# Matmuls without a use between the first attention units, and two expert weights asked for ahead of the attention's loop

## The chip, the cores and the metric

The kernel runs on one core of a Trainium2 chip. The metric is the device time of one execution in microseconds (us); the time before is the median of three runs. Beside it stands one execution taken by the hardware profiler, from which all rows below come. GB/s and MB are powers of ten, KB is 1024 bytes.

## What is computed

The reference has three stages. A linear attention with a decaying state runs over 4 batches, 8 heads, 768 positions and a head size of 48; its output, as 3072 tokens of 384 features, goes through a soft mixture of 8 experts with 4 slots each, and that through a feed-forward block with a squared ReLU.

```python
for t in range(S):                                   # attention, S = 768
    cur = np.einsum('bhd,bhe->bhde', u[None] * kt, vt)
    y[:, :, t] = np.einsum('bhd,bhde->bhe', rt, state + cur)
    state = w[None, :, :, None] * state + np.einsum('bhd,bhe->bhde', kt, vt)
...
logits = x @ phi                                     # experts: softmax over tokens in, over slots out
slot_input = softmax_over_tokens(logits).T @ x
slot_out[e] = np.maximum(slot_input[e] @ w1[e], 0.0) @ w2[e]     # 8 experts
x = softmax_over_slots(logits) @ slot_out
...
h = x @ w_in                                         # feed-forward, 384 -> 2048 -> 384
r = np.maximum(h, 0.0)
out = (r * r) @ w_out
```

## The kernel before

The order of the work is written out by hand: each engine, and SyncE's queue of transfers, runs its instructions in the order in which the program names them. The attention is cut into 16 units (one batch and two heads each; four units make a batch), each of 6 chunks of 128 positions. A unit's inputs come in four transfers: `load_t` brings the transposed keys and queries (two halves of 384 KB, line 92), `load_n` the natural keys, queries and values (448 and 416 KB, line 96, where the second half holds the rest of the queries and all values). There are four buffers for units (`NB = 4`), so unit n+4 is loaded into the buffer that unit n leaves; its loads are asked for at the end of iteration n, and each waits until TensorE has read what it overwrites. The first four units are asked for at the start, with the small `phi` between them. SyncE issues all of these transfers, and at most eight of them are under way: each waits also for the one eight places before it.

The work on unit n is: `bonus` (line 236 on, two GpSimd products; needs both halves of `load_n`), `decay` (line 232, VectorE, one for the keys, one for the queries), `weigh` (line 242, VectorE, needs the bonus), `keys` (line 248, GpSimd), `diag` (line 254, GpSimd, needs weigh), `A` (line 264, TensorE, two halves), `strict` (line 270, VectorE, copies A's result under a mask), `KV` (line 278, TensorE, needs keys), `scan` (line 283, VectorE), `Y` (lines 301 and 307, TensorE), and `X` and `L` (lines 320 and 335, TensorE: transposes and logits). An iteration n of the loop (line 440) runs A's second half and Y of unit n, keys, weigh, diag, KV, scan and A's first half of unit n+1, and bonus and the first decay of unit n+2. On GpSimd that is keys(n+1), two diags of n+1, bonus(n+2); on VectorE decay(n+1), strict(n) and so on stand behind weigh(n+1). "KV(5)" below is KV of unit 5; "strict(4,1)" is the second half of unit 4. In every fourth iteration a batch's softmax work (`soft_max` to `slots_norm`) is added.

The experts' weights are 16 transfers of 1536 KB each (`load_weight`, line 171 for w1 and 173 for w2). Nine of them have buffers of their own from the start (slots 4 to 12); they are asked for in the loop, each behind a unit's loads, in the iterations n = 0, 2, 3, 5, 6, 8, 9, 10, 11. The others follow as buffers come free: of the last units, and, behind the attention, of a pool ("post") that takes the place of the attention's tiles. There also stand the loads of w_in (line 137) and w_out (line 147). TensorE's last block, line 817, is the feed-forward's second product.

`keep_clock(n)` (line 220) is n matmuls of the identity with itself into a PSUM tile that nobody reads; each is two instructions on TensorE. It shares the tile of `X` (tag "tr", one buffer).

Of the kernel before, what the change touches and what calls it, by code (L numbers as in the profile page):

```python
# [29 lines left out]
def rwkv_softmoe_ffn(ctx: ExitStack, tc: tile.TileContext, tr, krv, wt, u, phi, w1, w2, w_in, w_out, out):  # L30
# [29 lines left out]
    def ps(tag):  # L60
        cnt[0] += 1
        return psum.tile([128, 512], F32, name=f"ps_{tag}{cnt[0]}", tag=tag, bufs=BANKS[tag])

    def wk(shape, tag, bufs, dt=F32, pool=None):
        cnt[0] += 1
        return (pool or work).tile(shape, dt, name=f"{tag}_{cnt[0]}", tag=tag, bufs=bufs)
# [3 lines left out]
    def take(i, dt=F32, cols=3072):  # L70
        cnt[0] += 1
        slots[i] = const.tile([128, SLOT[i]], dt, name=f"slot{i}_{cnt[0]}", tag=f"slot{i}", bufs=1)[:, :cols]
        return slots[i]
# [7 lines left out]
    def t_view(n):  # L81

        return units[n % NB][:112, :2 * S].rearrange("p (m c t) -> p m c t", m=2, c=NC)

    def n_view(n):

        return units[n % NB][:, 2 * S:].rearrange("p (m c h d) -> p m c h d", m=3, c=NC, h=2)
# [74 lines left out]
    def load_weight(i):  # L162
        kind, e = W[i]
        if str(home[i]).startswith("post"):
            cnt[0] += 1
            t = post.tile([128, 3072], F32, name=f"post_{cnt[0]}", tag=home[i], bufs=1)
        else:
            t = take(home[i])
        if kind == "w1":
            t = t.rearrange("p (c f) -> p c f", c=3)  # L170
            nc.sync.dma_start(t, w1[e].rearrange("(c p) f -> p c f", p=128))
        else:
            nc.sync.dma_start(t.rearrange("p (k f) -> p k f", k=3), w2[e].rearrange("k p f -> p k f"))
            t = t.rearrange("p (c d) -> p c d", c=8)
        wt_of[W[i]] = t
# [21 lines left out]
    for i in range(6):  # L197
        n = 1 << i
# [21 lines left out]
    def keep_clock(n):  # L220

        if n:
            p = ps("tr")
        for _ in range(n):
            nc.tensor.matmul(p[:, :256], ident, ident.unsqueeze(1).to_broadcast([128, 2, 128]), start=True, stop=True)


    def decay(n, m):

        x = t_view(n)[:, m]  # L230
        t = tab[:, n % NP] if m else tab[:, n % NP, ::-1]
        nc.vector.tensor_tensor(x, x, t.unsqueeze(1).to_broadcast([112, NC, 128]), ALU.mult)  # L232
# [7 lines left out]
    def weigh(n):  # L240
        dg = wk([128, NC, 2], "dg", 2)
        nc.vector.reduce_sum(dg, n_view(n)[:, 1], axis=AX.X)
        st[n, "dg"] = dg

    def keys(n, eng=nc.gpsimd):

        kv_ = n_view(n)[:, 0]
        eng.tensor_tensor(kv_, kv_, pkn[:, n % NP].unsqueeze(1).to_broadcast([128, NC, 2, D]), ALU.mult)

    def diag(n, g):  # L250
        at = wk([128, GC, 2, 128], "AT", 3, pool=att)
        st[n, "AT", g] = at
        dg = st[n, "dg"][:, GC * g:GC * (g + 1)]
        nc.gpsimd.affine_select(out=at.rearrange("p c h t -> p (c h) t"),  # L254
                                in_=dg.rearrange("p c h -> p (c h)").unsqueeze(2).to_broadcast([128, 2 * GC, 128]),
                                pattern=[[0, 2 * GC], [1, 128]], compare_op=ALU.is_equal, fill=0.0, base=0, channel_multiplier=-1)

    def A(n, g):
        tv = t_view(n)
        p = [ps("A")[:, :GC * 128].rearrange("p (c t) -> p c t", c=GC) for _ in range(2)]  # L260
        for i in range(GC):
            for h in range(2):
                rows = slice(64 * h, 64 * h + D)
                nc.tensor.matmul(p[h][:, i], tv[rows, 1, GC * g + i], tv[rows, 0, GC * g + i], start=True, stop=True)  # L264
        st[n, "A", g] = p

    def strict(n, g):
        at, p = st[n, "AT", g], st.pop((n, "A", g))
        for h in range(2):
            nc.vector.copy_predicated(at[:, :, h], mask.unsqueeze(1).to_broadcast([128, GC, 128]), p[h])  # L270
# [16 lines left out]
    def Y(n, g):  # L287
        vv, tv = n_view(n)[:, 2], t_view(n)
        at, s = st.pop((n, "AT", g)), SB[n % 2]

        p = [y.rearrange("p (c t) -> p c t", t=128) for y in yp]
        chunks = range(GC * g, GC * (g + 1))
        at_of = lambda c, j: p[c % 2][64 * j:64 * j + D, (c - chunks[c % 2 != chunks[0] % 2]) // 2]
        opened = set()
        for c in chunks:
            for h in range(2 if c > 0 else 0):
                rows, j = slice(64 * h, 64 * h + D), (h + c) % 2  # L300
                nc.tensor.matmul(at_of(c, j), s[rows, c], tv[rows, 0, c],  # L301
                                 start=(c % 2, j) not in opened, stop=True, skip_group_check=True)
                opened.add((c % 2, j))
        for c in chunks:
            for j in range(2):
                h = (j + c) % 2
                nc.tensor.matmul(at_of(c, j), vv[:, c, h], at[:, c - GC * g, h],  # L307
                                 start=False, stop=True, skip_group_check=True)
        if g == 0:
            st[n, "xT"] = wk([112, NC, 128], "xT", 2, pool=att)  # L310
        for k in range(2):
            c0 = chunks[k]
            nc.scalar.copy(st[n, "xT"][:, c0:GC * (g + 1):2], p[c0 % 2][:112, :len(chunks[k::2])])  # L313
# [34 lines left out]
    def soft_exp(b):  # L348

        eT = wk([96, 2, 256], "eT", 1)  # L350
        st["eT", b] = eT
        nc.scalar.activation(eT[:, 0], st["lg", b][:96, :256], AF.Exp, bias=st["nm", b])
        nc.scalar.copy(eT[:, 1], st["lg", b][:96, :256])
        if 0 < b < B - 1:
            new = st["new", b]
            fa, fb = wk([96, 1], "fa", 2), wk([96, 1], "fb", 2)
            nc.scalar.activation(fa, nmx[:, 0:1], AF.Exp, bias=new, scale=-1.0)
            nc.scalar.activation(fb, st["nm", b], AF.Exp, bias=new, scale=-1.0)
            nc.scalar.copy(nmx[:, 0:1], new)
            st["f", b] = fa, fb  # L360
# [56 lines left out]
    bonus(0)  # L417
    decay(0, 1)
    decay(0, 0)
    keep_clock(6)  # L420

    pp = ps("lg")
    for a in range(NP):
        nc.tensor.transpose(pp[:, a * 128:a * 128 + 112], tabs[:, a], ident[:112, :112])
    nc.scalar.copy(pkn, pp.rearrange("p (a b d) -> p a b d", a=NP, b=2)[:, :, :, :D])
    A(0, 0)
    weigh(0)
    diag(0, 0)
    keys(0, nc.vector)
# [6 lines left out]
        nc.gpsimd.memset(xn[i][:, :, DM:DM + 1], 1.0)  # L436
    bonus(1)
    decay(1, 0)
    nload = 0
    for n in range(NU):  # L440
        nxt = n + 1 < NU
        if n == 2:

            sel = const.tile([128, 4, NS], F32, name="sel")
            nc.vector.reduce_sum(sel, ident.rearrange("p (q s) -> p s q", q=4).unsqueeze(1).to_broadcast([128, 4, NS, 4]), axis=AX.X)
            rm = const.tile([128, E], F32, name="rm")
            nc.vector.reduce_sum(rm, ident.rearrange("p (q e j) -> p e q j", q=4, e=E), axis=AX.XY)
            ones = const.tile([1, 4], F32, name="ones")
            nc.gpsimd.memset(ones, 1.0)

        b, j = divmod(n, NP)
        b -= 1
        A(n, 1)
        if nxt:
            keys(n + 1)
            weigh(n + 1)
            diag(n + 1, 0)
            decay(n + 1, 1)
        strict(n, 1)
        if n > 0:  # L460
            X(n - 1, 0)
        if b >= 0 and j == 1:
            soft_exp(b)
        Y(n, 0)
        if b >= 0 and j == 2:
            soft_sum(b)
            slots_exp(b)
        if nxt:
            KV(n + 1)
            diag(n + 1, 1)  # L470
        if n > 0:
            L(n - 1)

        if nxt:
            A(n + 1, 0)
            scan(n + 1)
            strict(n + 1, 0)
        if n > 0:
            X(n - 1, 1)
        if not nxt:  # L480
            L(n, (0,))
            X(n, 0)
        Y(n, 1)
        if b >= 0 and j == 1:
            soft_turn(b)
        if n + 2 < NU:
            bonus(n + 2)
            decay(n + 2, 0)
        if b >= 0 and j == 0:
            soft_max(b)  # L490
        if b >= 0 and j == 2:
            slots_norm(b)
        if n + NB < NU:
            load_t(n + NB)
            load_n(n + NB)
            if n not in (1, 4, 7):
                load_weight(nload)
                nload += 1
        elif n == NU - 2:
            load_win(0)  # L500
        else:
            load_weight(nload)
            nload += 1
# [382 lines left out]
```

## Time and profile before

| | |
|---|---|
| time, median of 3 runs | 401.37 us (400.80 to 401.72) |
| the profiled execution, its own time | 400.18 us |
| its span, first to last instruction | 398.5 us |
| mean granted TensorE clock | 0.973 |
| TensorE busy | 381.7 us (96% of the span) |
| VectorE busy | 280.2 us (70%) |
| ScalarE busy | 211.7 us (53%) |
| GpSimd busy | 114.8 us (29%, nearly all in the first 120 us) |
| transfers | 70.81 MB, mean 178 GB/s over the span |

PE is TensorE's matmuls, PEld its weight loads, DVE VectorE, ACT ScalarE, POOL GpSimd, SP SyncE; SPq is SyncE's sequencer, which issues the transfers. L264 is line 264 of the kernel. Times inside the trace count from the span's start. Matmuls are pipelined and their ends are modelled, so a TensorE that is busy throughout is not one at its peak. The span runs to the last instruction; the execution's own time is 1.7 us longer.

### The profile page before, as it was taken

To read this page: it belongs to the slowest core of one execution; us is meant where nothing else is said; L and a number is where in the kernel's file an instruction comes from. 1 tells how busy PE (TensorE), PEld (TensorE's weight loads), DVE (VectorE), ACT (ScalarE), POOL (GpSimd) and SP (SyncE) were. 2 spreads that over 40 slices of the span, in tenths; PEclk is the share of its full clock that TensorE was granted. 3 is DMA by queue.
4 is the path that set the end of the run, shared out by engine and by line. 5 is a ranking of instruction groups with operands and counts; after the bars stand their busy time and mean duration, and the time that the engine had idled before them with its cause. 6 is when DMAs were issued, how large, how long until landed. Compare 5 with 4: busy or idle time off the path is not lost.

```text
span 398.5 us, 8194 instructions
## 1 busy us (share of the span) xinstructions
PE 381.7 (96%) x3219; PEld 294.2 (74%) x3219; DVE 280.2 (70%) x495; ACT 211.7 (53%) x465; POOL 114.8 (29%) x110
## 2 busy tenths in 40 slices
PE   5799999999999999789999999999999999999995
PEld 3677777767766564668787888888888888888884
DVE  5769897879974564799998567666566676566563
ACT  2224453453444451678888876555554564554552
POOL 3869997986870001122323120000000000000000
PEclk8559999999999999999999999999999999999999
DMA  7999999999995899913333202100000040000004
GB/s 245 344 320 343 389 407 403 404 404 406 405 383 188 307 410 405 375 47 102 85 100 87 63 0 104 56 0 2 0 0 2 0 159 2 0 0 2 0 0 158
DMA packets 25989, 70.81 MB, mean 178 GB/s; under 512 B 3680, under 2 KB 6112, under 8 KB 25952
## 3 DMA queue, kind: packets, MB, share of 16 engines
q1 hardware_dynamic: 25808, 70.10, 47.2%
q10 hardware_dynamic: 144, 0.20, 0.5%
q8 instruction: 25, 0.41, 0.4%
q14 instruction: 12, 0.10, 0.1%
HBM read 64.78 MB, written 4.72 MB: 174 GB/s over the span
## 4 chain that ended last, share of the span: by engine, by line
PE 80%; DMA 9%; DVE 6%; POOL 2%; issue 1%; ACT 1%; SPq 0%; POOLq 0%; ACTq 0%; DVEq 0%
PE ps_Y L817 16%; PE ps_A L817 16%; PE ps_kv L817 8%; PE ps_lg L817 8%; PE ps_A L264 7%; DMA wo<-in_w_out_dram 7%; PE ps_Y L307 5%; PE ps_Y L301 3%; PE ps_tr L320 3%; PE ps_tr L725 3%; PE ps_tab L725 3%; PE ps_lg L335 2%; DMA slot<-in_krv_dram 2%; PE ps_kv L278 2%; PE ps_tr L378 1%
## 5 line engine op out<-in xcount | busy, mean ns | idle before, releaser
L817 PE MATMUL ps_Y<-slot,slot 128*128 128x512 f32 x288 | 111.7, 395 | 0.0
L750 DVE TENSOR_TENSOR slot<-gg,slot 128x512 fp32r<-128x512 f32 (+1 forms) x97 | 66.5, 685 | 49.2 <-ACT slot L747 48.3
L817 PE MATMUL ps_A<-slot,slot 128*128 128x512 f32 x288 | 88.9, 393 | 0.6 <-DVE slot L682 0.6
L747 ACT CAST slot<-gg 128x512 fp32r<-128x512 f32 (+1 forms) x97 | 59.8, 618 | 50.5 <-DVE gg L744 49.9
L817 PEld LDWEIGHTS ps_A<-slot,slot 128*128 128x128 f32 x288 | 54.0, 188 | 13.2 <-DVE slot L682 1.0
L817 PEld LDWEIGHTS ps_Y<-slot,slot 128*128 128x128 f32 x288 | 54.1, 188 | 12.6 <-issue 0.6
L744 DVE TENSOR_TENSOR gg<-hr 128x512 f32<-128x512 f32 (+1 forms) x71 | 49.0, 691 | 14.3 <-ACT hr L737 14.2
L817 PE MATMUL ps_kv<-slot,slot 128*128 128x512 f32 x144 | 55.7, 394 | 0.0
L817 PE MATMUL ps_lg<-slot,slot 128*128 128x512 f32 x144 | 55.4, 391 | 0.0
L623 POOL TENSOR_TENSOR slot<-wf,slot 128x384 fp32r<-128x384 f32 x16 | 19.1, 1196 | 97.5 <-ACT slot L618 97.5
L270 DVE COPY_PREDICATED AT<-mask,ps_A 128x384 f32<-128x384 int32 x64 | 33.8, 583 | 9.2 <-PE ps_A L264 8.4
L264 PE MATMUL ps_A<-slot 48*128 48x128 f32 x384 | 36.2, 310 | 2.9 <-DVE slot L232 1.8
L264 PEld LDWEIGHTS ps_A<-slot 48*128 48x128 f32 x384 | 28.7, 204 | 10.3 <-DVE AT L270 3.6
L737 ACT ACTIVATE hr<-ps_tab 128x512 f32<-128x512 f32 x48 | 28.7, 599 | 12.9 <-PE ps_tab L725 12.9
L737 ACT ACTIVATE hr<-ps_tr 128x512 f32<-128x512 f32 (+1 forms) x49 | 28.8, 590 | 12.4 <-PE ps_tr L725 12.4
L313 ACT COPY xT<-ps_Y 112x256 f32<-112x256 f32 x64 | 17.4, 324 | 28.0 <-PE ps_Y L307 27.8
L254 POOL TENSOR_SCALAR_AFFINE_SELECT AT<-dg 128x768 f32<-128x768 f32 x32 | 28.0, 886 | 13.2 <-PE ps_Y L307 8.4
L817 PEld LDWEIGHTS ps_kv<-slot,slot 128*128 128x128 f32 x144 | 27.1, 188 | 6.2
L817 PEld LDWEIGHTS ps_lg<-slot,slot 128*128 128x128 f32 x144 | 27.0, 188 | 5.9
L232 DVE TENSOR_TENSOR slot<-slot,ps_tab 112x768 f32<-112x768 f32 x32 | 30.1, 941 | 0.6 <-DMA slot<-in_tr_dram 0.6
L307 PE MATMUL ps_Y<-AT,slot 128*48 128x128 f32 x384 | 29.6, 293 | 0.0
L307 PEld LDWEIGHTS ps_Y<-AT,slot 128*48 128x48 f32 x384 | 20.8, 129 | 6.5 <-issue 5.9
(168 smaller groups left out, 502.3 us busy)
## 6 DMA issues: line engine op xcount, KB each, us to landing
slot<-in_w_dram SPq DMA_DIRECT2D x14, 1536.0 KB, 11.1
slot<-in_tr_dram SPq DMA_DIRECT2D x32, 384.0 KB, 7.5
slot<-in_krv_dram SPq DMA_DIRECT2D x16, 448.0 KB, 7.3
slot<-in_krv_dram SPq DMA_DIRECT2D x16, 416.0 KB, 7.8
slot<-in_w_in_dram SPq DMA_DIRECT2D x4, 1536.0 KB, 19.1
wo<-in_w_out_dram SPq DMA_DIRECT2D x16, 384.0 KB, 3.3
out_dram<-os SPq DMA_DIRECT2D x15, 256.0 KB, 2.2
post<-in_w_dram SPq DMA_DIRECT2D x2, 1536.0 KB, 9.2
```

What stands on the lines that cost most here:

```text
L232: nc.vector.tensor_tensor(x, x, t.unsqueeze(1).to_broadcast([112, NC, 128]), ALU.mult)
L254: nc.gpsimd.affine_select(out=at.rearrange("p c h t -> p (c h) t"), in_=dg.rearrange("p c h -> p (c h)").unsqueeze(2).to_broadcast([128, 2 ...
L264: nc.tensor.matmul(p[h][:, i], tv[rows, 1, GC * g + i], tv[rows, 0, GC * g + i], start=True, stop=True)
L270: nc.vector.copy_predicated(at[:, :, h], mask.unsqueeze(1).to_broadcast([128, GC, 128]), p[h])
L307: nc.tensor.matmul(at_of(c, j), vv[:, c, h], at[:, c - GC * g, h], start=False, stop=True, skip_group_check=True)
L623: nc.gpsimd.tensor_tensor(wout_half(wls, f, WL), st.pop(("wf", f)), hi, ALU.subtract)
L725: nc.tensor.matmul(p, gst[:, 128 * f:128 * (f + 1)], cTall[:, 512 * g:512 * (g + 1)], start=True, stop=True)
L737: nc.scalar.activation(fs[i, "hr"][:, c], fs[i, "p"][:, c], AF.Relu)
L744: nc.vector.tensor_mul(gg, hr, hr)
L747: nc.scalar.copy(part(i, "gh")[:, c], fs[i, "gg"][:, c])
L750: nc.vector.tensor_tensor(part(i, "gl")[:, c], fs[i, "gg"][:, c], fs[i, "gh"].bitcast(F32)[:, c], ALU.subtract)
L817: nc.tensor.matmul(o, (hi, lo, hi)[k][:, 128 * j:128 * (j + 1)], (gh, gh, gl)[k], start=(f == 0 and k == 0), stop=(f == NF - 1 and k == 2))
```

## The change

Two things change. Five calls of `keep_clock` are added or made larger: 16 instead of 6 matmuls ahead of the first transposes, 4 ahead of A of unit 0, 3 ahead of weigh(0) (on TensorE: between A's first half and KV of unit 0), and in iteration 0 of the loop 3 ahead of Y and 4 behind it. And the first two weights are asked for ahead of the loop, behind the loads of units 0 to 3 in SyncE's queue; in the loop a weight is then asked for in the iterations n = 0, 2, 4, 6, 8, 10, 11. The number of weights, their order and their buffers are the same.

```diff
     decay(0, 1)
     decay(0, 0)
-    keep_clock(6)
+    keep_clock(16)
...
     nc.scalar.copy(pkn, pp.rearrange("p (a b d) -> p a b d", a=NP, b=2)[:, :, :, :D])
+    keep_clock(4)
     A(0, 0)
+    keep_clock(3)
     weigh(0)
...
     bonus(1)
     decay(1, 0)
-    nload = 0
+    for nload in range(2):
+        load_weight(nload)
+    nload = 2
     for n in range(NU):
...
             X(n - 1, 0)
         if b >= 0 and j == 1:
             soft_exp(b)
+        if n == 0:
+            keep_clock(3)
         Y(n, 0)
+        if n == 0:
+            keep_clock(4)
...
         if n + NB < NU:
             load_t(n + NB)
             load_n(n + NB)
-            if n not in (1, 4, 7):
+            if n not in (1, 3, 5, 7, 9):
                 load_weight(nload)
                 nload += 1
```

## Rows read from the trace of the kernel before

**Rows 1.** The page's 40 slices of 9.96 us each: granted clock in tenths, GB/s.

```profile
PEclk8559999999999999999999999999999999999999
...
GB/s 245 344 320 343 389 407 403 404 404 406 405 383 188 307 410 405 375 47 102 85 100 87 63 0 104 56 0 2 0 0 2 0 159 2 0 0 2 0 0 158
```

**Rows 2.** Busy time by stretch: from:to, length, then the columns of the heading.

```profile
core 0: us, PE busy (x) PEld busy (x) DVE busy (x) ACT busy (x) POOL busy (x), PEclk, DMA share, GB/s
18.80:28.30 9.50, 9.44 (x93) 7.51 (x95) 6.36 (x11) 1.91 (x7) 6.66 (x7) 0.50 0.90 324
44.92:51.07 6.15, 6.15 (x109) 4.82 (x107) 5.22 (x9) 2.64 (x9) 5.89 (x6) 1.00 1.02 402
22.90:31.00 8.10, 8.10 (x102) 6.33 (x100) 4.43 (x8) 2.31 (x9) 4.97 (x6) 0.66 0.85 299
31.00:37.00 6.00, 6.00 (x104) 4.60 (x96) 5.75 (x11) 2.16 (x9) 5.42 (x6) 1.00 1.02 398
37.00:40.00 3.00, 3.00 (x43) 2.29 (x42) 2.89 (x5) 1.36 (x5) 2.84 (x3) 1.00 0.67 233
60.00:110.00 50.00, 49.38 (x801) 36.66 (x797) 42.31 (x72) 22.49 (x79) 41.16 (x35) 1.00 1.03 405
...
40.00:44.00 4.00, 4.00 (x81) 3.17 (x79) 3.01 (x6) 1.98 (x7) 3.75 (x5) 1.00 1.01 373
```

**Rows 3.** GpSimd in order of time: start, us, line, tiles [idle before, releaser].

```profile
28.58 0.87 POOL L254 TENSOR_SCALAR_AFFINE_SELECT AT<-dg 128x768 f32<-128x768 f32 x1 [2.97 <-PE ps_Y L307]
...
36.00 1.41 POOL L237 TENSOR_TENSOR slot<-slot,U 128x576 f32<-128x576 f32 x1
...
42.22 1.41 POOL L237 TENSOR_TENSOR slot<-slot,U 128x576 f32<-128x576 f32 x1
...
45.20 1.42 POOL L248 TENSOR_TENSOR slot<-slot,pkn 128x576 f32<-128x576 f32 x1
...
61.55 1.42 POOL L237 TENSOR_TENSOR slot<-slot,U 128x576 f32<-128x576 f32 x1 [0.16 <-DMA slot<-in_krv_dram]
...
82.27 1.42 POOL L237 TENSOR_TENSOR slot<-slot,U 128x576 f32<-128x576 f32 x1
```

**Rows 4.** SyncE's queue in order of time: issue, us on the sequencer, line, transfer.

```profile
16.59 0.43 SPq L92 DMA_DIRECT2D slot<-in_tr_dram  x1
...
17.12 5.90 SPq L92 DMA_DIRECT2D slot<-in_tr_dram  x2
...
32.33 0.38 SPq L96 DMA_DIRECT2D slot<-in_krv_dram  x1
...
133.56 0.90 SPq L173 DMA_DIRECT2D post<-in_w_dram  x2
```

**Rows 5.** The chain that ended last, 133 to 176 us: start, us, what.

```profile
139.99 14.27 DMA wo<-in_w_out_dram
```

**Rows 6.** TensorE at the start, in order of time.

```profile
1.43 4.36 PE L225 MATMUL ps_tr<-ident 128*128 128x256 f32 x12 [1.43 <-POOL ident masks.py:199]
8.57 1.01 PE L424 MATMUL ps_lg<-ident,xT 112*128 112x112 f32 x4 [2.79 <-ACT xT L210]
...
4.54 1.24 PE L225 MATMUL ps_tr<-ident 128*128 128x256 f32 x5
```

**Rows 7.** TensorE in order of time: Y of unit 1, then unit 4's iteration.

```profile
26.98 1.52 PE L307 MATMUL ps_Y<-AT,slot 128*48 128x128 f32 x12
...
47.28 0.62 PE L278 MATMUL ps_kv<-slot 128*48 128x48 f32 x20
...
48.40 0.94 PE L264 MATMUL ps_A<-slot 48*128 48x128 f32 x12
...
50.27 0.86 PE L307 MATMUL ps_Y<-AT,slot 128*48 128x128 f32 x12
```

**Rows 8.** Transfers issued at 16.59 and at 32.33: KB, us to landing.

```profile
slot<-in_tr_dram SPq DMA_DIRECT2D x1, 384.0 KB, 7.8
...
slot<-in_krv_dram SPq DMA_DIRECT2D x1, 416.0 KB, 6.7
```

**Rows 9.** VectorE in unit 4's iteration, in order of time.

```profile
46.69 1.06 DVE L270 COPY_PREDICATED AT<-mask,ps_A 128x384 f32<-128x384 int32 x2
```

## The prediction, before the changed kernel was run

> **What bounds the kernel now.** I read the slices of the page first, for where TensorE's clock is low and where the transfers fill their engines; then busy time by stretch; then the order of one attention unit on GpSimd, TensorE and VectorE; then SyncE's queue and what each transfer takes to land; last the chain behind the attention.
>
> The slices show the low clock in the second and third slice, about 8 to 28 us, and some 400 GB/s of transfers from the fifth slice on [rows 1]. By stretch: from 18.80 to 28.30 the granted clock is 0.50 (1.2 GHz) though TensorE counts 9.44 us busy of 9.50; later it is 1.00 (2.4 GHz), and unit 4 takes 6.15 us from one A to the next (44.92 to 51.07), with TensorE busy throughout and GpSimd 5.89 us of it [rows 2]. So a unit in steady state is paced by TensorE, with GpSimd 0.26 us behind.
>
> Transfers don't pace the loop yet, but they are close. GpSimd starts unit 5's bonus at 42.22, 6.22 us after unit 4's (36.00) and with no wait; unit 8's is the only bonus in the loop that waited for data, 0.16 us [rows 3]. Behind the attention the kernel is one block tied to its end: SyncE asks for the first weights of the freed pool at 133.56, as soon as the last soft_sum has run, and the chain goes on with a wait of 14.27 us for a piece of w_out that is queued behind those weights [rows 4, 5]; TensorE runs the last block after them. None of the transfers there is asked for earlier by this change. So whatever moves the attention's end moves the time by as much, and the question is how long 16 units take.
>
> **Part 1: the matmuls without a use.** 24 more calls, two instructions each on TensorE: 48. Before, 12 took 4.36 us while the clock rose, 0.36 each; the last five took 1.24 us, 0.25 each [rows 6]. So they add 12 to 17 us of TensorE time, nearly all of it in waits. In the first call, 20 more instructions run from 5.8 to about 10.1 (they start 0.21 to 0.25 us apart at the full clock): over the idle 2.79 us before the transposes of 8.57 [rows 6], and 1.5 us past it. Followed on through the next calls at full clock I get KV(0) at 14.6 and KV(1) at 20.4, each about 1.6 us later than now, but A(1,0) ends at 21.9, where it ends now (21.6), and Y(1,0) ends near 25.8 instead of 28.5. GpSimd gets this: its diag at 28.58 waited 2.97 us for that Y [rows 3], so unit 3's bonus and all behind it could start some 2.7 us earlier, and unit 4's at 33.3 instead of 36.00. Cost on the path: nothing; cover: the waits for GpSimd's chain. Possible gain: 2.7 us, if data are there.
>
> The size of the clock's effect, from rows at both levels: twelve matmuls of Y took 1.52 us at 0.50 and 0.86 at 1.00 [rows 7], 1.77 times as much.
>
> **Part 2: the two weights.** No bytes are added. Ahead of unit n+4's load there are now more weights than before: two more for units 4 to 7 (unit 4: two instead of none; unit 5: three instead of one; unit 7: four instead of two), one or two more to unit 13, none for 14 and 15. All go through SyncE's one queue, in its order. Two things are gained: the queue has work where it now waits for TensorE to free a buffer (the pair of unit 4's transfers that begins at 17.12 takes SyncE 5.90 us) [rows 4], and the engines fill the stretches of 299 and 233 GB/s (22.9 to 31 and 37 to 40) [rows 2]. What is lost: units 4 to 7 stand behind 3.15 MB.
>
> When does unit 5 land? Unit 3's last piece is asked for at 16.59 and lands 7.8 us later, at 24.4 [rows 4, 8]. Nothing in front of it changes. Behind it stand, up to unit 5's last piece: three weights (1536 KB each, 1.573 MB) and two units (448 + 416 + 2 x 384 = 1632 KB, 1.671 MB), 8.06 MB in all. The nearest full stretch (31 to 37) moves 398 GB/s; the best long one (60 to 110) 405; a slow one (40 to 44) 373 [rows 2]. At 398 it lands 20.25 us later, at 44.6; the bounds are 44.3 and 46.0. I take 398 because it is the same mixture at the same time. Now it lands at 32.33 + 6.7 = 39.0 [rows 4, 8], 3.2 us ahead of its need.
>
> What a late unit 5 costs: its bonus starts at 44.6 instead of 42.22, 2.4 us late. The cover: unit 5's keys end at 46.62 (45.20 + 1.42) and KV(5) starts at 47.28 [rows 3, 7]; VectorE's strict(4,1), queued behind weigh(5), ends at 47.75 and the next A starts at 48.40 [rows 7, 9]. Both leave 0.65 us. So TensorE is late by 2.4 - 0.65 = 1.75 us. As TensorE has no idle time per unit, it doesn't win this back; unit 8's wait of 0.16 us goes at most. Net: +1.7 us; with the bounds on landing +1.3 to +3.0.
>
> The same sum for the others. Unit 4: 4.82 MB, 36.5 against a need of 36.00: within the cover, but the possible 33.3 of part 1 is lost. Unit 7: 12.98 MB, 57.0, against its own bonus, now at 42.22 + 2 x 6.15 = 54.5 and shifted by 2.4 to 56.9: no more. Unit 11: six weights and eight units, 22.81 MB at 405 GB/s, 80.7, against its bonus at 82.27 [rows 3]: early, by 1.6 us only. From unit 12 on the data are early by more. Profiled time 400.18 us (span 398.5 and 1.7 around it) becomes 401.9; the median of the runs, 401.37, lies 1.2 us above that execution, and I add the 1.7 to the median: 403.1 us.
>
> The Trainium skill ("DMA: Bandwidth & Descriptors", section "Rules for kernel authors") says to issue a transfer early and wait late, since its setup is then hidden. By it alone the two weights would cost nothing and part 1's 2.7 us would stay: the faster rival below. This case's rows speak against it: at 398 to 405 GB/s over long stretches the queue is full, and a transfer issued early is a place taken [rows 2].
>
> **Rivals.**
> Faster: the early lead passes on. TensorE is 2.7 us ahead, the transfers never pause, and unit 5 comes in time. It decides at unit 5's landing: with the cover, 42.9 is no loss, which needs 8.06 MB in 18.5 us, 436 GB/s; no long stretch exceeds 405 [rows 2]. Unit 11 caps it: not before 80.7, so 1.6 + 0.65 = 2.2 us at best, 399.2 us.
> No difference: the wait for unit 5 is there, but the queue catches up nearly a us (engines that finish early take the weights' pieces sooner), or the cover is larger because TensorE's order gives way elsewhere. 401.4, within 0.8 us.
> Slower by more: the clock falls in the new waits. TensorE, warm and ahead, would wait for unit 4's data and again for unit 5's, about 2 us each. In this trace the clock falls in the second slice, in which TensorE stands still from 5.8 to 8.57, and stays at 0.50 into the third although TensorE is counted busy [rows 1, 2, 6]. One unit at 0.50 costs up to 6.15 x 0.77 = 4.7 us (0.77: the excess of Y, 1.52 against 0.86 [rows 7]); if the clock falls at unit 4, the wait for unit 5 hides 1.75 of this. So 1.7 + 3.0, 406.1 us; with the fall at unit 5 408, and with half a unit at 0.50 some 404.5. Against it: from the fourth slice on the clock stays up to the end [rows 1]; but TensorE hardly waits there (49.38 us busy of 50 [rows 2]), so these rows don't try it.
> The Trainium skill ("TensorE: Matmul & The Clock Gate", section "HAM oscillation — how this bites in real kernels") describes this rival: a wait for data between bursts of matmuls throttles TensorE again, and the next burst starts at half rate. The fall in the second slice agrees; no row here shows one in the loop.
> The change doesn't do what it says: the clock still falls near 8 to 12. Then part 1's lead is gone, but unit 4 has 2.7 + 0.5 us to spare before its data, so the sum stays that of the forecast; I give it no chance of its own.
>
> **How the numbers follow.** Forecast (unit 5 late, 402.4 to 404.4): 0.52. Clock falls (404.4 to 408): 0.20. No difference: 0.17. Faster: 0.11. The median can tell about 0.2%, 0.8 us, from no change. Slower is 0.52 + 0.20 = 0.72, same 0.17, faster 0.11. For the range I leave out most of the faster case (0.10), the lower edge of no difference (0.04) and the clock's upper end (0.06): 401.0 to 406.2.
>
> **What would show it.** Part 1: granted clock 1.00 from 5 to 28 us and Y(1,0) ending by 26. Part 2: GB/s near 400 from 20 to 44 without the dips; unit 5's last piece landing near 44.6; GpSimd's bonus of unit 5 (line 237, the sixth) waiting for a krv transfer by about 2 us, and of unit 4 by up to 3; KV(5) near 49.0. The end of the attention 1.7 us later (the freed pool's first weight asked for near 135.3), and all behind it unchanged in length. Wrong, if unit 5 lands before 43, if the loop's pace falls below 6.15 us a unit, or if the block behind the attention changes its length.

## The result, and the profile after

The changed kernel takes 405.56 us (median of eight executions, 402.51 to 408.38), the kernel before 401.44 (eight, 399.85 to 402.97): 1.0098 times as long [1.0069, 1.0127]. It is slower, as forecast, inside the forecast's range, and 2.5 us above its 403.1. It lies outside the bounds of the forecast's own case (402.4 to 404.4) and inside those of its rival "the clock falls" (404.4 to 408).

The eight executions fall into two groups by the mean granted clock. Three have 0.996 or 0.997: 402.51, 402.65 and 404.34 us. Five have 0.983 to 0.987: 405.55, 405.56, 406.74, 407.85 and 408.38. The profiled one is the 406.74, with a span of 405.0 and 0.987. Its slices (granted clock in tenths, GB/s) answer to [rows 1]:

```profile
PEclk9999689999999999999999999999999999999999
...
GB/s 248 328 409 413 408 335 365 362 341 350 361 340 221 259 417 416 408 102 63 120 75 110 63 3 78 79 2 0 0 2 0 0 158 1 0 2 0 0 2 155
```

The low clock of the start has gone. A new one stands in the fifth and sixth slice, in the attention's loop, and the third to fifth slices are full of transfers. Busy time by stretch, with the columns of [rows 2]:

```profile
18.80:28.30 9.50, 9.50 (x153) 7.58 (x151) 7.29 (x12) 2.96 (x10) 8.57 (x9) 1.00 1.00 388
22.90:31.00 8.10, 8.10 (x142) 6.40 (x142) 7.37 (x12) 3.80 (x12) 7.12 (x8) 1.00 1.03 419
31.00:37.00 6.00, 6.00 (x102) 4.47 (x98) 5.75 (x10) 2.10 (x7) 2.69 (x3) 1.00 1.03 412
...
39.50:42.00 2.50, 0.00 (x0) 0.00 (x0) 1.46 (x2) 0.54 (x2) 2.42 (x3) 1.00 1.04 420
44.00:54.00 10.00, 10.00 (x102) 7.37 (x100) 5.23 (x8) 2.64 (x10) 6.88 (x6) 0.50 1.03 405
```

The first line is what the matmuls without a use were to do: the granted clock is 1.00 where it was 0.50. The fourth is a stretch in which TensorE runs nothing at all. In the fifth it runs throughout, at half the clock. GpSimd, in order of time (start, us, line, tiles, idle before and releaser; [rows 3]):

```profile
27.61 1.41 POOL L237 TENSOR_TENSOR slot<-slot,U 128x576 f32<-128x576 f32 x1
...
37.62 1.41 POOL L237 TENSOR_TENSOR slot<-slot,U 128x576 f32<-128x576 f32 x1 [3.40 <-DMA slot<-in_krv_dram]
...
40.58 1.40 POOL L248 TENSOR_TENSOR slot<-slot,pkn 128x576 f32<-128x576 f32 x1
...
45.40 1.41 POOL L237 TENSOR_TENSOR slot<-slot,U 128x576 f32<-128x576 f32 x1 [1.78 <-DMA slot<-in_krv_dram]
...
48.36 1.41 POOL L248 TENSOR_TENSOR slot<-slot,pkn 128x576 f32<-128x576 f32 x1
```

Unit 3's bonus (27.61) is 1.8 us earlier than before, when it stood at 29.41. Unit 4's bonus then waits 3.40 us for its data, and unit 5's 1.78 us. TensorE in the same time ([rows 7]):

```profile
25.84 0.86 PE L307 MATMUL ps_Y<-AT,slot 128*48 128x128 f32 x12
...
38.63 0.86 PE L307 MATMUL ps_Y<-AT,slot 128*48 128x128 f32 x12
42.04 0.66 PE L278 MATMUL ps_kv<-slot 128*48 128x48 f32 x20 [2.55 <-POOL slot L248]
42.62 0.64 PE L335 MATMUL ps_lg<-xT,phs 112*32 112x128 f32 x12
43.19 1.25 PE L264 MATMUL ps_A<-slot 48*128 48x128 f32 x12
...
46.15 1.52 PE L307 MATMUL ps_Y<-AT,slot 128*48 128x128 f32 x12
...
51.85 1.01 PE L278 MATMUL ps_kv<-slot 128*48 128x48 f32 x20
52.79 1.08 PE L335 MATMUL ps_lg<-xT,phs 112*32 112x128 f32 x12
53.80 0.97 PE L264 MATMUL ps_A<-slot 48*128 48x128 f32 x12
...
58.87 0.62 PE L278 MATMUL ps_kv<-slot 128*48 128x48 f32 x20
```

The three L278 lines are KV of units 4, 5 and 6. Ahead of KV(4) TensorE stands for 2.55 us; some 1.6 us after it has started again the same instructions take longer (Y 1.52 instead of 0.86), until about 53.9. KV(5) waits for nothing: its keys end at 49.77 (48.36 + 1.41), 2.1 us before TensorE gets to it. KV(4) and KV(6) of the kernel before, whose KV(5) is in [rows 7]:

```profile
41.13 0.62 PE L278 MATMUL ps_kv<-slot 128*48 128x48 f32 x20
...
53.43 0.62 PE L278 MATMUL ps_kv<-slot 128*48 128x48 f32 x20
```

From these lines the sum of this execution can be made. KV(4) is 0.91 us later (42.04 against 41.13). From KV(4) to KV(5) it is 9.81 us instead of 6.15, 3.66 more; from KV(5) to KV(6) 7.02 instead of 6.15, 0.87 more. That makes 5.44 us. SyncE's queue asks for the freed pool's first weights so much later ([rows 4]: 133.56), and the wait for w_out behind it is as long as before ([rows 5]: 14.27):

```profile
138.99 0.90 SPq L173 DMA_DIRECT2D post<-in_w_dram  x2
```
```profile
145.41 14.12 DMA wo<-in_w_out_dram
```

So some 5.4 of the span's 6.5 us have arisen when unit 6 begins. Not all of the 4.53 (3.66 + 0.87) behind KV(4) are the clock's: unit 5's keys end at 49.77, and KV(5) stood at 47.28 before, so its late data alone would have cost 2.5 us in this execution. The fall adds the 2.1 us by which TensorE gets to KV(5) after the keys, and the 0.87 behind it, together 2.9. The other 1.1 lie behind the attention: from the pool's request to the end it is 264.9 us before and 266.0 here. Between 264.5 and 266.4 it came out so in every profile below, without an order that goes with the change.

### The profile page after: what moved, and what is told of

Its sections match the earlier page's. It is cut to its first block, busy times and chain, and to the rows that moved or that the text cites. A ratio compares the mean times of both kernels' runs of the same rounds, so it can differ in the third digit from the quotient of the medians.

```text
span 405.0 us, 8291 instructions
## 1 busy us (share of the span) xinstructions
PE 391.2 (97%) x3267; PEld 300.8 (74%) x3267; DVE 280.2 (69%) x495; ACT 211.4 (52%) x465; POOL 113.6 (28%) x110
## 4 chain that ended last, share of the span: by engine, by line
PE 80%; DMA 11%; DVE 5%; POOL 1%; issue 1%; ACT 1%; SPq 0%; POOLq 0%; DVEq 0%; ACTq 0%
PE ps_A L825 16%; PE ps_Y L825 16%; PE ps_kv L825 8%; PE ps_lg L825 8%; DMA wo<-in_w_out_dram 7%; PE ps_A L264 6%; PE ps_Y L307 4%; PE ps_tr L225 4%; DMA slot<-in_krv_dram 3%; PE ps_Y L301 3%; PE ps_tab L733 3%; PE ps_tr L733 3%; PE ps_tr L320 3%; PE ps_lg L335 2%; PE ps_kv L278 2%; PE ps_tr L378 1%
## 5 line engine op out<-in xcount | busy, mean ns | idle before, releaser
L631 POOL TENSOR_TENSOR slot<-wf,slot 128x384 fp32r<-128x384 f32 x16 | 18.1, 1131 | 98.6 <-ACT slot L626 98.6
L264 PE MATMUL ps_A<-slot 48*128 48x128 f32 x384 | 33.8, 298 | 0.8 <-DVE AT L270 0.8
L264 PEld LDWEIGHTS ps_A<-slot 48*128 48x128 f32 x384 | 26.5, 192 | 8.2 <-DVE AT L270 3.5
L237 POOL TENSOR_TENSOR slot<-slot,U 128x576 f32<-128x576 f32 x16 | 22.5, 1408 | 11.2 <-DMA slot<-in_krv_dram 11.2
## 6 DMA issues: line engine op xcount, KB each, us to landing
post<-in_w_dram SPq DMA_DIRECT2D x2, 1536.0 KB, 10.1
```

The lines of the kernel that those rows point to most:

```text
L237: nc.gpsimd.tensor_tensor(rv, rv, U[:, n % NP].unsqueeze(1).to_broadcast([128, NC, 2, D]), ALU.mult)
```

## The experiments

Two theories were to be told apart. By the first, the early weights make units 4 and 5 late, as forecast, and in part of the executions the clock falls in the waits that this opens; the waits cost 1.5 to 2 us and the fall the rest. By the second, the matmuls without a use, or the later weights' new places, cost time of their own. Every kernel below computes all of the reference. Ratios are against the kernel before, run on the same chip.

**The matmuls alone** (e1). The changed kernel with the weights where they were:

```diff
-    for nload in range(2):
-        load_weight(nload)
-    nload = 2
+    nload = 0
...
-            if n not in (1, 3, 5, 7, 9):
+            if n not in (1, 4, 7):
```

> The calls of keep_clock as in the changed kernel, the weights in the places of the kernel before. Theory 1 (the place of the two weights is the whole cost; the matmuls without a use alone bring TensorE some 2.7 us ahead): granted clock 1.00 from about 6 us on with no fall, unit 5's last piece landing at about 39 and no wait for it, unit 8 again near its landing; 1 to 2.7 us faster than the kernel before. Theory 2 (the matmuls without a use cost time at the start): slower than before by 1 to 5 us, with KV(1) and what follows late by as much.

Measured: 398.65 against 400.74 us, 0.9947 [0.9920, 0.9973]. The profile has the granted clock at 1.00 from the start to the end of the attention, and unit 5's bonus and KV(5), both without a wait, 2.6 us earlier than in [rows 3, 7]; the pool is asked for at 130.93:

```profile
39.58 1.41 POOL L237 TENSOR_TENSOR slot<-slot,U 128x576 f32<-128x576 f32 x1
```
```profile
44.65 0.62 PE L278 MATMUL ps_kv<-slot 128*48 128x48 f32 x20
```

So the matmuls without a use, taken together, bring 2.1 us in the median, 2.6 at the attention's end. The second theory's first half falls. Two of the twelve executions have a mean clock of 0.989 and 0.990, the others 0.997 or more; both took 400.96 us, 2.3 above the median. The clock seems to fall now and then in this kernel too, in which the weights stand where they did; no trace shows where.

**The weights alone** (e2). The kernel before with the two weights ahead of the loop and the new places:

```diff
-    nload = 0
+    for nload in range(2):
+        load_weight(nload)
+    nload = 2
...
-            if n not in (1, 4, 7):
+            if n not in (1, 3, 5, 7, 9):
```

> The two weights ahead of the loop and the places of the others as in the changed kernel, keep_clock as before. Theory 1: units 4 and 5 land at about 37.5 and 45.3 as in the changed kernel; TensorE, which has no lead here, waits under 1 us for unit 4 and about 2 us for unit 5; 2 to 2.7 us slower than before, and up to 5 if the clock falls in the wait for unit 5. Theory 2: no difference from before.

Measured: 402.35 against 400.74 us, 1.0037 [1.0014, 1.0059], +1.6 in the median. Unit 4 needs its data at 35.94 and has them; unit 5 hasn't:

```profile
43.89 1.42 POOL L237 TENSOR_TENSOR slot<-slot,U 128x576 f32<-128x576 f32 x1 [1.70 <-DMA slot<-in_krv_dram]
```
```profile
48.32 0.66 PE L278 MATMUL ps_kv<-slot 128*48 128x48 f32 x20 [0.93 <-POOL slot L248]
```

TensorE waits 0.93 us, KV(5) is 1.04 late (48.32 against 47.28), and the pool is asked for 1.1 us late (134.64). The clock stays at 1.00 from 30 to 110 us. This is the forecast's mechanism by itself. Its size is below the 2 to 2.7 us expected here: unit 4 had no wait, and unit 5's bonus starts at 43.89 instead of 45.3. From KV(5) to the pool's request nothing is added (1.04 and 1.1 late), so the second theory's other half, a cost of the later weights' new places, doesn't show. Added up, the two parts alone make -2.1 + 1.6 = -0.5 us; together they measured +4.1. The 4.6 us between come from the two parts meeting.

**Work in the new waits** (e3). The changed kernel with matmuls without a use in the two waits, so that TensorE never stands:

```diff
+            keep_clock({3: 6, 4: 4}.get(n, 0))
             KV(n + 1)
```

> The changed kernel with six more calls' worth of matmuls without a use ahead of KV(4) and four ahead of KV(5), so that TensorE isn't idle while it waits for the late units. Theory 1 (of the changed kernel's loss some 1.5 us are the late units and the rest the clock's fall in the wait): the clock stays at 1.00 through the loop, KV(4) and KV(5) start no earlier than 42.0 and about 49.8, and the time is 1 to 2 us over the kernel before, 3 us under the changed kernel's profiled execution. Rival (the late units cost it all, the clock only shows it): no faster than the changed kernel.

Measured: 404.66 us, 1.0092 [1.0063, 1.0122]. The mean clock is 1.000 in five of the six executions and 0.993 in one, and they lie within 404.14 and 404.75. The scatter went, the median hardly moved. The profile shows why: the filling was too long.

```profile
39.47 2.86 PE L225 MATMUL ps_tr<-ident 128*128 128x256 f32 x12
42.26 0.65 PE L278 MATMUL ps_kv<-slot 128*48 128x48 f32 x20
...
48.54 1.99 PE L225 MATMUL ps_tr<-ident 128*128 128x256 f32 x8
50.46 0.65 PE L278 MATMUL ps_kv<-slot 128*48 128x48 f32 x20
```

The keys ended at 40.83 and 48.61 here, so the fillings held KV(4) back by some 1.4 us and KV(5) by 1.8. The time expected, 1 to 2 us over the kernel before, was missed: it is 3.9 over. In the profile KV(5) is 3.2 us late, of which 1.8 are the filling, and the pool is asked for 3.2 late (136.79). So the run can't tell its two theories apart by the time; it says that with the stands filled the mean clock is 1.000 in five executions of six.

**A smaller filling** (e5), three matmuls and one:

```diff
+            keep_clock({3: 3, 4: 1}.get(n, 0))
             KV(n + 1)
```

> The changed kernel with three more calls of keep_clock ahead of KV(4) and one ahead of KV(5), 1.3 and 0.4 us of matmuls, short enough to end before the units' keys do. Theory 1 (in the changed kernel the late units cost 1.0 to 1.7 us and the clock's fall in the wait for unit 4 the rest): no fall in the loop, KV(4) within 0.2 us of the end of unit 4's keys and KV(5) of unit 5's, 1.2 to 2 us slower than before, and the times of single executions as close as those of the weights alone. Rival (the late units cost it all): 4 us slower than before, as with the longer filling.

Measured: 402.64 against 400.83 us, 1.0044 [1.0029, 1.0058]. Nine of ten executions have a mean clock of 0.997 to 1.000 and take 402.16 to 403.19 us. That is 1.8 us over the kernel before, about what the weights alone cost (1.6), and close to two of the changed kernel's three executions with a high mean clock (402.51 and 402.65; the third took 404.34). The tenth is the profiled one, 409.41 us, which the ratio leaves out; for it the expectation of no fall was missed. There unit 5's data came later (bonus at 45.03), TensorE stood 1.82 us, and the clock fell:

```profile
47.60:49.50 1.90, 0.08 (x3) 0.06 (x4) 1.56 (x3) 0.04 (x1) 1.82 (x3) 1.00 1.01 403
49.90:60.10 10.20, 10.20 (x96) 7.57 (x92) 6.07 (x11) 2.71 (x9) 6.19 (x6) 0.50 0.97 332
```

So one kernel has both outcomes. An execution of it that was profiled on another chip (e9) had no fall:

> The shorter filling once more, for a profile of an execution in which the clock doesn't fall (nine of ten executions had a mean clock of 0.997 or more): KV(5) starts 4.4 us after unit 5's bonus, at 49 to 50, the freed pool's first weight is asked for near 135.2, 1.6 us later than in the kernel before, and all behind it has the same length.

It took 403.52 us with a mean clock of 1.000; the bonus of unit 5 began at 44.19 and the pool was asked for at 136.11, 0.9 us later than expected. On that chip the early lead was missing (last section), so the filling ahead of KV(4) stood in TensorE's way: KV(4) starts at 42.85, 2.0 us after unit 4's keys end. KV(5) and KV(6) of the two executions, first with the fall (e5), then without (e9):

```profile
49.45 0.69 PE L278 MATMUL ps_kv<-slot 128*48 128x48 f32 x20 [1.82 <-POOL slot L248]
...
60.13 0.64 PE L278 MATMUL ps_kv<-slot 128*48 128x48 f32 x20
```
```profile
49.76 0.66 PE L278 MATMUL ps_kv<-slot 128*48 128x48 f32 x20
...
55.95 0.62 PE L278 MATMUL ps_kv<-slot 128*48 128x48 f32 x20
```

Up to KV(5) they are level; to KV(6) the one takes 10.68 us, the other 6.19. So the fall costs 4.5 us there. A second fall of the first one comes behind the attention, in the 14th slice of its page:

```profile
PEclk9999959999999899999999999999999999999999
```

By half microseconds it lies from about 138.7 to 142.1 us. From 130 us on the longest stand of TensorE ahead of it is 0.55 us (up to 137.81), and the kernel before has the same stand before the same instruction (up to 131.05) and keeps its clock. It costs 1.3 us up to the pool's request (141.61, 81.5 us after KV(6), against 80.2 in e9).

**A longer wait** (e8). No weight ahead of the loop, and three behind unit 4's loads, so that unit 4 is in time and unit 5 very late:

```diff
-    for nload in range(2):
-        load_weight(nload)
-    nload = 2
+    nload = 0
...
-            if n not in (1, 3, 5, 7, 9):
+            for _ in range((3, 0, 1, 0, 1, 0, 1, 0, 1, 0, 1, 1)[n]):
                 load_weight(nload)
                 nload += 1
```

> keep_clock as in the changed kernel, the two weights asked for behind unit 4's loads (three weights in iteration 0) instead of ahead of them; all units from 5 on have the same bytes ahead as in the changed kernel. Theory 1 (unit 5 alone sets the loss, unit 4's lateness only takes the lead): unit 4 in time, KV(4) near 38.5, unit 5's last piece at about 45 and KV(5) at 49 to 50, after a wait of TensorE of 4 to 5 us in which the clock falls: 3 to 5 us slower than before. Rival (unit 4's place is the loss): faster than before by 1 us or more.

Measured: 410.13 us, 1.0226 [1.0191, 1.0262], 9.3 us over the kernel before where 3 to 5 were expected. The profiled execution is the fastest of the six (406.52, mean clock 0.989). In it unit 4's bonus starts at 34.55 without a wait and unit 5's at 46.72, 1.7 us later than expected. KV(5) waits 5.13 us, and the clock falls inside the wait:

```profile
51.13 1.04 PE L278 MATMUL ps_kv<-slot 128*48 128x48 f32 x20 [5.13 <-POOL slot L248]
```
```profile
46.00:47.80 1.80, 0.00 (x1) 0.00 (x0) 0.00 (x0) 0.54 (x2) 1.08 (x1) 1.00 1.04 418
47.80:54.60 6.80, 3.47 (x44) 2.82 (x44) 3.34 (x5) 0.63 (x1) 6.56 (x7) 0.50 1.03 407
```

All six executions have a mean clock of 0.989 or less; the five without a trace have 0.979 to 0.983 and took 409.89 us or more, so they were at the low clock for longer. The three weights ahead of unit 5 are the same in number as in the changed kernel; only their place against unit 4 differs. So a late unit 5 is enough for a loss, and a late unit 4 isn't needed for it. It doesn't show that unit 4 is harmless: in the changed kernel's profiled execution the fall came behind the wait for unit 4.

**One weight ahead** (e6):

```diff
-    for nload in range(2):
-        load_weight(nload)
-    nload = 2
+    load_weight(0)
+    nload = 1
...
-            if n not in (1, 3, 5, 7, 9):
+            if n not in (1, 3, 5, 7):
```

> keep_clock as in the changed kernel; one weight ahead of the loop instead of two, the others in the iterations 0, 2, 4, 6, 8, 9, 10, 11. Theory 1 (the landing of unit 5 decides): one weight less ahead is 3.9 us earlier; unit 4 lands near 32.5, before its need at 33.4, unit 5 near 41, some 1.5 us after its need at 39.6, so TensorE keeps 1 to 2 of the 2.6 us that the matmuls alone bring: 0.5 to 1.8 us faster than before, no fall of the clock. Rival (any weight ahead spoils the lead): no faster than before.

Measured: 398.95 us, 0.9954 [0.9938, 0.9970]. Unit 5's last piece lands at 40.14, half a us before its bonus (40.66, no wait); no fall. Most of what the matmuls alone bring (1.9 of 2.1 us) is there with one weight ahead, and it is lost with two.

**The weights later instead of earlier** (e4, e7). Both have the changed kernel's matmuls and no weight ahead of the loop. e4 asks for a weight in all iterations but n = 1, 3 and 5; e7 for none in n = 1, 3, 5 and 7 and for two in n = 11.

```diff
-            if n not in (1, 3, 5, 7, 9):
+            if n not in (1, 3, 5):
```

> keep_clock as in the changed kernel, no weight ahead of the loop, and the weights in the iterations 0, 2, 4 and from 6 on, so that no unit has more weights ahead of it than in the kernel before, and units 8 to 13 one fewer. Theory 1: no unit's landing gates the loop and TensorE's lead of 2.7 us reaches the end: 2 to 3 us faster than before, at least as fast as the matmuls alone. Rival (the loop gives the lead back, being paced by GpSimd and VectorE): within 1 us of before.

> keep_clock as in the changed kernel, no weight ahead, and the weights in the iterations 0, 2, 4, 6, 8, 9, 10 and two in 11, one later than in the other order for units 12 to 15. Theory 1: no unit from 2 on waits for data; the attention ends 2.6 to 3.2 us earlier than before and the time is 2.5 to 3.5 us less; the ninth weight lands later but ahead of its use behind the attention. Rival (the last weights, pushed back, hold the block behind the attention): as the matmuls alone or slower.

Measured: e4 397.17 us, 0.9911 [0.9878, 0.9944]; e7 398.20 us, 0.9933 [0.9911, 0.9955]. e4 beats both kernels. Its pool is asked for at 130.78, 2.8 us earlier than before. It doesn't come free: units 12 to 15 now wait for data, and late in the loop TensorE has a wait of its own:

```profile
107.25 0.66 PE L278 MATMUL ps_kv<-slot 128*48 128x48 f32 x20 [1.14 <-POOL slot L248]
```

The lead wasn't given back by this. The expectation's count was off: units 8, 10 and 11 have one weight fewer ahead of them than before, the others as many. In e7 unit 7's bonus waits 0.47 us for data, and the pool is asked for at 131.73, 1.8 us earlier than before where 2.6 to 3.2 were expected. Between e1, e4 and e7 the times differ by less than the intervals can order with certainty.

**The changed kernel once more** (e10), for a second trace of it:

> The changed kernel once more, for a second profile. With the clock's fall (mean clock 0.987): as the first, 405 to 408 us, TensorE's stretch at half clock beginning after the wait for unit 4 or for unit 5. Without it (0.996 or more): 402.5 us, KV(5) at about 49.7, the freed pool's first weight asked for near 135.3.

Measured: 403.15 us, one execution, mean clock 1.000. It is another chip, on which the kernel before took 404.26 in its one execution; the pair says nothing on the ratio, and only the trace is used. GpSimd, TensorE and SyncE:

```profile
36.49 1.41 POOL L237 TENSOR_TENSOR slot<-slot,U 128x576 f32<-128x576 f32 x1 [0.20 <-DMA slot<-in_krv_dram]
...
44.27 1.42 POOL L237 TENSOR_TENSOR slot<-slot,U 128x576 f32<-128x576 f32 x1 [1.75 <-DMA slot<-in_krv_dram]
```
```profile
48.70 0.66 PE L278 MATMUL ps_kv<-slot 128*48 128x48 f32 x20 [0.98 <-POOL slot L248]
```
```profile
135.02 0.90 SPq L173 DMA_DIRECT2D post<-in_w_dram  x2
```

The early lead had been lost for another reason (last section), unit 4 hardly waited, and in the loop TensorE stood for 0.98 us only. KV(5) is 1 us earlier than the 49.7 expected for this run. The prediction's numbers for unit 5's landing, KV(5) and the pool were 44.6, 49.0 and 135.3; here they are 44.2, 48.70 and 135.02.

## Why the prediction was right, and where its size was off

The direction and the range were right, and the late unit 5 behind them is shown by the runs. The number came out inside the range with some luck: the median lies in the bounds of the rival "the clock falls", not in those of the forecast's own case, and the range held it because most of that rival had been left in.

**What bounds the kernel**: right. In the eight experiments' profiles without a fall between KV(5) and the pool's request, a shift at KV(5) is found again at the pool's request within 0.4 us; where the clock fell, more was added. The block behind the attention took 264.5 to 266.4 us, a spread of 1.9 us, so that single profiles tell nothing about smaller differences there.

**Part 1, at no cost, a lead of 2.7 us**: right in kind. Y(1,0) ends at 26.7 in the changed kernel (25.84 + 0.86), where the forecast had 25.8; the lead at unit 3's bonus is 1.8 us instead of 2.7. In e1 it is 2.6. What differs is the length of the first call's 32 instructions, 9.48 us here and 8.66 in e1 (the forecast had them end near 10.1; they end at 10.90 and 10.08): in both the transposes start behind them without a wait, here at 10.74 though their input was ready at 8.95. Why the same call takes 8.66 to 9.83 us in the profiles isn't shown. The forecast's words that the first twelve ran "while the clock rose" are a misreading: by half microseconds the granted clock of the kernel before is 1.00 up to 7.5 us, and the first slice's 8 comes from the fall behind that.

**Part 2, unit 5 lands at 44.6**: right within 0.8 us. In the profiles with two weights ahead its bonus starts behind its data at 43.89 (e2), 44.19 (e9), 44.22 (e3), 44.27 (e10), 45.03 (e5) and, in the profiled execution of the changed kernel, 45.40. Four of the six lie below the forecast's lower bound of 44.3. Unit 4's bonus starts between 35.80 and 36.49 in the other five, as forecast (36.5), and at 37.62 in the profiled execution of the changed kernel, although its transfers moved faster than the forecast took, 419 and 412 GB/s for 398; why both units were about 1.1 us later there than in e10 isn't shown.

**The cost at TensorE, 2.4 - 0.65 = 1.75 us**: the sum is right, its size was about 0.7 too high. The delay of the bonus in e2 is 1.67 (43.89 - 42.22), less the cover of 0.65 gives 1.02, and KV(5) was 1.04 late. Where the clock stays up, the changed kernel takes 402.51 to 404.34 us and e5 402.64 in the median, with 403.1 forecast. And part 1's lead is worth nothing then, as the forecast had it: with unit 5's data late, it doesn't matter when TensorE is ready. The Trainium skill ("DMA: Bandwidth & Descriptors", section "Rules for kernel authors") says to issue a transfer early, since its setup is then hidden. For these two weights that brought no gain: e2 issues them earlier and changes nothing else but the later weights' places, and costs 0.37%.

**The clock's fall, 0.20**: this is the term that was mis-sized, by its chance. The forecast knew the mechanism, its place (unit 4, if the lead held) and its price (406.1 us, or 404.5 to 408; the five executions with a low clock took 405.55 to 408.38). It gave this case a chance of 0.20 and left it out of the 403.1; by the mean clock five of the eight executions have the fall, and so the median does. In the profiled execution the late data cost 2.5 us and the fall 2.9 up to unit 6, where the rival had 1.7 and 3.0. The argument against it was that the clock stays up from the fourth slice of the kernel before on; the text itself said that TensorE hardly waits there. The right inference from that was that those rows are no evidence either way. The row that did bear on it was the fall in the second slice, around a stand of 2.79 us [rows 6], and the forecast itself expected two new stands of about 2 us each. The Trainium skill ("TensorE: Matmul & The Clock Gate", section "HAM oscillation — how this bites in real kernels") has a wait for data between bursts of matmuls throttle TensorE again; the fifth stretch after the change agrees, 10.00 us at 0.50 behind a stand of 2.55.

Why both parts together lose more than the sum of each: the matmuls make TensorE arrive 1.8 us sooner at data that the weights make later, and the two add up in the length of the wait. Of the 4.6 us between, 2.1 are the lead, which late data make worthless; the other 2.5 go with the clock's fall. With the weights alone TensorE stood 0.93 us and the clock held. In the changed kernel it stood 2.55, in e5's profiled execution 1.82, in e8 5.13, and the clock fell; in e10 it stood 0.98 in the loop and 1.69 ahead of the first transposes (10.97 to 12.66), and it held both times. So in the loop the longer stands are the ones with a fall, and filling them goes with fewer executions of low mean clock, one in ten (e5) and at most one in six (e3, the 0.993) instead of five in eight, though not all on the same chip. That the length of the stand decides is argued, not shown, and it can't be all: e5's second fall came behind stands of at most 0.55 us, and two executions of e1 have a low mean clock without a late unit 5. What makes the same kernel fall in one execution and not in the next was not shown: for the executions without a fall at the usual start there is no trace.

**The rivals**: "slower by more" is what the median shows. Faster fell with unit 5's landing, which was never near 42.9 with two weights ahead, and was possible with one (e6) or none. No difference fell by the interval. What would show it wrong was named as a landing before 43, a loop faster than 6.15 us a unit, or a block of another length. The first two didn't come; the block is 1.1 us longer in the profiled execution, within the spread of all profiles.

## What to carry to other kernels

When the transfers fill their queue, an early request is paid for by whatever stands behind it: count the bytes ahead of the next piece that is needed, and move requests until that piece lands just in time. Two changes can meet in one wait, if one brings the consumer forward and the other sets its data back; the wait's length then has to be judged as that of a TensorE that stands, with a fall of the clock as a possible outcome. When one kernel has executions of two kinds, compare their mean clocks before explaining the median. And a stretch in which an engine never waits says nothing about what its clock does in a wait.

## What was not expected

In e10 (and in e9, on the same chip) one small transfer, the decay's base, landed some 2.3 us later: VectorE waited 4.17 us for it in e10, against 1.89 in the kernel before. That moved VectorE's products for the decay table beside GpSimd's first bonus, and there they took 1.24 and 1.30 us. In the kernel before, ahead of that bonus, the same two took 0.29 and 0.43. First the lines of e10, then of the kernel before:

```profile
8.70 1.41 POOL L237 TENSOR_TENSOR slot<-slot,U 128x576 f32<-128x576 f32 x1 [5.82 <-DMA slot<-in_krv_dram]
...
9.01 1.24 DVE L199 TENSOR_TENSOR P<-P,pw 112x128 f32<-112x128 f32 x1
...
10.57 1.30 DVE L199 TENSOR_TENSOR P<-P,pw 112x256 f32<-112x256 f32 x1
```
```profile
6.73 0.29 DVE L199 TENSOR_TENSOR P<-P,pw 112x128 f32<-112x128 f32 x1
...
7.34 0.43 DVE L199 TENSOR_TENSOR P<-P,pw 112x256 f32<-112x256 f32 x1
```

The transposes that need the table start at 12.66 there, against 10.74 in the profiled execution of the changed kernel. That was enough to undo the early lead: unit 3's bonus is at 29.69, against 29.41 in the kernel before. That running beside GpSimd's product is what made the two slower is argued from these rows only. Why the transfer was late on that chip stays open.
